# Handing out a feed-forward layer item by item between attention cells, with per-pair loads and weight casts on another engine

## The chip, the cores and the metric

The kernel runs on one core of a Trainium2 chip. The metric is the device time of one execution in microseconds (us). TensorE (PE in the profile) does matrix products, with its weight loads listed apart as PEld; VectorE is DVE, ScalarE is ACT, GpSimd is POOL, and SyncE (SP) issues most of the transfers. SBUF is the memory on the core that the engines read and write, divided into 128 partitions; PSUM is the memory into which TensorE writes its results. Times come from several executions; a profile comes from one execution, and its span is about 2 us shorter than the device time of the same run.

Each run is labelled with a state. On one core a run counts as slow when it is more than 1.5% above the fastest run of the same kernel. Ratios in this document are the mean time of one kernel's fast runs over the mean time of the other kernel's fast runs in the same rounds, so they are not quite the ratio of the medians quoted beside them. Intervals are 95% intervals.

## The reference, cut to what matters

Two layers follow each other. The first is a block-wise linear attention with a decaying state, for 4 batches, 8 heads, 768 positions and head size 64. The second is a dense feed-forward layer over all 3,072 tokens.

```
for b in range(nb):                         # blocks of one sequence, in order
    intra = (qb @ kb^T) * Dmask @ vb         # within the block
    inter = (qb * lam_pow) @ kv_state        # from all earlier blocks
    out[block] = intra + inter
    kv_state = lam_block * kv_state + (kb * rev_pow)^T @ vb

h = x @ w_in                                 # x: 3072 x 512, w_in: 512 x 2048
g = 0.5 * h * (1 + tanh(c * (h + 0.044715 h^3)))
return g @ w_out                             # w_out: 2048 x 512
```

The only serial dependency is `kv_state`, from one block to the next of the same head. Each group of 512 tokens of the feed-forward layer needs all eight heads of its tokens, and nothing else of the attention.

## The kernel before

The kernel uses blocks of 128 tokens (six for each batch) and works on two heads at a time, a "head pair" of 128 partitions (four pairs). I call one block of one head pair a cell; there are 4 x 6 x 4 = 96 cells. Everything is computed in 16-bit floats and accumulated in 32 bits in PSUM. Here `Sps` holds the products of k and q, `PT` is their masked form, `OKV` holds the output and the update of the state, and `xT` is the attention output that the feed-forward layer reads. This is one cell, cut:

```python
Sps = ps_S.tile(...)                               # 2 buffers
# two matmuls: k^T q of each head                  -> Sps
nc.vector.tensor_tensor(PT, Sps, mask, ALU.mult)   # DVE
OKV = ps_OKV.tile([P, P + D], FP32, tag="OKV")     # 2 buffers
for hl in range(2):                                # two heads
    nc.tensor.matmul(OKV[opart, 0:P], a16[v], PT, ...)
    if blk > 0:
        nc.tensor.matmul(OKV[opart, 0:P], kv_prev, qkT, ...)
    nc.tensor.matmul(OKV[opart, P:P+D], a16[k], a16[v], ...)
# DVE: kv32_new, kv_new = decay * kv32_prev + OKV[:, P:P+D]
# ACT: xT[:, hp, tokens] = OKV[:, 0:P]
```

The feed-forward group of 512 tokens has 16 first-layer steps (I call one an item) and four second-layer blocks of 16 matmuls each. `Hps` and `O2ps` are the PSUM results of the two layers, and `gT` holds the activated first layer of a group:

```python
gT = gt_pool.tile([P, NF, GSZ], FP16, tag="gT")    # 16 KiB per partition, 1 buffer
for f in range(16):
    # 4 matmuls 128x128 by 512 columns           -> Hps  (2 PSUM buffers, shared with O2ps)
    # ACT h = Hps;  DVE s = h*h;  DVE u = (s+C)*h;  ACT z = sigmoid(u);  DVE gT[f] = z*h
for tau in range(4):
    # 16 matmuls over gT and w_out               -> O2ps ; ACT o = O2ps ; store
```

And this is the order in which the program hands the work to the engines, cut:

```python
# w_in's 4 MB load is issued first, then q, k, v of batch 0
groups_after_batch = {0: [0], 1: [1, 2], 2: [3], 3: [4, 5]}
for b in range(B):
    qkv_next = load_qkv(b + 1)
    for hp in range(NHP):
        attention_hp(b, hp, *qkv_cur)        # all six blocks of a pair, one after the other
        if b == 0 and hp == 0:
            emit_w_out_load_cast()           # one 4 MB load, 16 casts on ACT
    for g in groups_after_batch[b]:
        emit_moe_group(g)                    # whole groups
```

## Time and profile before

| | before |
|---|---|
| median of 4 runs | 410.97 us (410.69 to 411.7) |
| span of the profiled run | 409.0 us |
| first cell of batches 0, 1, 2 and 3 (its Sps matmul), from the timeline | 31.3, 80.0, 163.7 and 255.2 us |
| last cell | 320.5 us |
| first gT | 114.7 us |
| from the last cell's Sps to the end ("the tail") | 88.4 us |

The page of the profile of the kernel before: busy time of each engine, then the span in 40 slices of about 10.2 us each, a digit being the busy share of the slice in tenths; PEclk is the clock granted to PE in tenths of full speed.

```profile
PE 308.6 (75%) x1696; PEld 144.4 (35%) x1696; DVE 232.0 (57%) x658; ACT 193.5 (47%) x388; POOL 17.5 (4%) x41
...
PE   0015989797278898889987999977988975895585
...
DVE  3023465546289907995389805999044568518840
...
PEclk9999999999999999999999996899995569999999
```

No engine is full on average. PE has three gaps: the start (first three digits), the slice with digit 2 at about 105 us, and the fives in the last quarter. DVE swings between 9 and 0 or 3 from slice to slice. So the kernel is a series of stages with different limits, and not one stage with one limit.

Stretches of the kernel before. Columns: stretch in us, its length, then busy time (and count of instructions) of PE, PEld, DVE, ACT and POOL, the granted PE clock, the busy share of the DMA engines, and GB/s.

```profile
40.00:50.00 10.00, 9.41 (x58) 4.73 (x57) 4.17 (x17) 3.25 (x10) 0.96 (x2) 1.00 1.14 218
100.00:110.00 10.00, 1.38 (x12) 1.05 (x11) 1.65 (x4) 9.51 (x19) 0.78 (x2) 1.00 0.77 157
120.00:130.00 10.00, 8.68 (x53) 4.14 (x51) 9.29 (x26) 6.69 (x15) 0.00 (x0) 1.00 0.00 0
140.00:150.00 10.00, 9.53 (x45) 4.09 (x44) 3.90 (x10) 2.55 (x5) 0.00 (x0) 1.00 0.21 73
310.00:320.00 10.00, 7.86 (x53) 4.32 (x52) 4.89 (x19) 3.07 (x8) 0.00 (x0) 0.50 0.00 0
340.00:350.00 10.00, 5.66 (x24) 2.32 (x24) 8.60 (x18) 6.66 (x12) 0.00 (x0) 1.00 0.01 2
```

At 100–110 us PE stands still while ACT casts w_out. At 120–130 us DVE is the limit, at 140–150 us PE is and DVE idles. At 340–350 us, in the tail, PE has only 24 matmuls (six items) in 10 us, and DVE is 86% busy. At 310–320 us nearly only attention runs (the first wide matmul comes at 319.75 us), and the granted clock is half.

The timeline of PE in the kernel before. Columns: start in us, duration in us, engine, line of the program, operation with output and inputs, shapes; in brackets the idle time before it and what ended it.

```profile
71.86 0.31 PE L174 MATMUL OKV<-qkT,kv_new 64*64 64x128 f16 x1 [0.29 <-DVE kv_new L184]
...
73.42 0.31 PE L174 MATMUL OKV<-qkT,kv_new 64*64 64x128 f16 x1 [0.29 <-DVE kv_new L184]
...
75.91 0.61 PE L203 MATMUL Hps<-xT,w_in 128*128 128x512 f16 x1
...
129.31 0.24 PE L174 MATMUL OKV<-qkT,kv_new 64*64 64x128 f16 x1
...
318.83 0.31 PE L174 MATMUL OKV<-qkT,kv_new 64*64 64x128 f16 x1 [0.29 <-DVE kv_new L184]
```

Consecutive blocks of one pair come every 1.56 us, and each time PE stands 0.29 us until DVE has made the new state. The last two lines give a second reading: the same matmul takes 0.31 us at 72 us and 0.24 us at 129 us, and a wide matmul takes 0.61 us here and 0.38 us later. At 319 us, where the granted clock reads 0.50, it takes 0.31 us again. The Trainium skill, "TensorE: Matmul & The Clock Gate", Part 1, says that the PE clock is at half rate by default (1.2 instead of 2.4 GHz) and that activity releases it. The durations (0.31 and 0.24 us) agree with two such speeds.

Two lines of the waits of the kernel before. Columns: who waits, for whom, us in total, times, longest.

```profile
ACT o L222 <- PE O2ps L219: 56.3, 24, 2.9
...
PE OKV L174 <- DVE kv_new L184: 11.8, 27, 0.9
```

### The profile page before, as it was taken

The page shows a single profiled execution, that of the slowest core. Times are in us where ns is not written, and L with a number is a line of the kernel's source. Part 1 is how long each engine was busy: PE and PEld are TensorE (multiplying, and loading weights), DVE is VectorE, ACT ScalarE, POOL GpSimd, SP SyncE. Part 2 cuts the span into 40 slices and gives each one's busy share as a digit, 9 for nine tenths or more (in the row PEclk, how much of TensorE's full clock was granted, in tenths as well). Part 3 has the DMA queues.
Part 4 walks back from the last instruction along what each step waited for, and adds up shares of the span by engine and source line. Part 5 has one row for each costly group of instructions (what it writes and reads, how often), then busy time and mean ns, then how long its engine had stood idle before and what let it go on. Part 6 is the DMA issues. An engine that isn't in the chain of part 4 may idle for free.

```text
span 409.0 us, 4938 instructions
## 1 busy us (share of the span) xinstructions
PE 308.6 (75%) x1696; PEld 144.4 (35%) x1696; DVE 232.0 (57%) x658; ACT 193.5 (47%) x388; POOL 17.5 (4%) x41
## 2 busy tenths in 40 slices
PE   0015989797278898889987999977988975895585
PEld 0002444353034344344443444343444322342232
DVE  3023465546289907995389805999044568518840
ACT  3512222333967616773467433576133266436641
POOL 1001011101000001000000101010010000000000
PEclk9999999999999999999999996899995569999999
DMA  7999999980950054001100020000200000020002
GB/s 286 283 217 218 218 258 338 220 171 2 207 101 2 1 147 111 0 2 39 63 2 2 3 101 0 2 0 2 78 26 2 0 0 2 26 77 2 2 26 78
DMA packets 24841, 33.87 MB, mean 83 GB/s; under 512 B 752, under 2 KB 19184, under 8 KB 24304
## 3 DMA queue, kind: packets, MB, share of 16 engines
q1 hardware_dynamic: 24816, 33.56, 33.1%
q8 instruction: 13, 0.21, 0.2%
q14 instruction: 12, 0.10, 0.1%
HBM read 27.27 MB, written 6.29 MB: 82 GB/s over the span
## 4 chain that ended last, share of the span: by engine, by line
PE 48%; DVE 21%; issue 11%; ACT 10%; POOLq 0%; POOL 0%; ACTq 0%; DVEq 0%
PE O2ps L219 16%; PE Hps L203 11%; DVE u L211 8%; PE OKV L174 7%; PE OKV L176 6%; DVE s L209 4%; ACT h L207 3%; PE Tps L149 3%; PE OKV L171 3%; ACT z L214 2%; DVE kv_new L181 2%; ACT w_out L120 2%; DVE gT L215 2%; PE Sps L163 2%; DVE PT L166 2%
## 5 line engine op out<-in xcount | busy, mean ns | idle before, releaser
L203 PE MATMUL Hps<-xT,w_in 128*128 128x512 f16 x384 | 104.9, 407 | 23.2 <-ACT h L207 23.0
L219 PE MATMUL O2ps<-w_out,gT 128*128 128x512 f16 x384 | 84.9, 379 | 4.8 <-ACT h L207 3.9
L214 ACT ACTIVATE z<-u 128x512 f16<-128x512 f16 x96 | 59.9, 629 | 45.8 <-DVE u L211 45.7
L211 DVE SCALAR_TENSOR_TENSOR u<-s,h 128x512 f16<-128x512 f16 x96 | 65.4, 692 | 1.2
L203 PEld LDWEIGHTS <-w_in 128*128 128x128 f16 x384 | 36.5, 100 | 67.1 <-issue 33.7
L189 ACT ACTIVATE xT<-OKV 128x128 f16<-128x128 f32 x96 | 26.4, 275 | 70.9 <-DVE kv_new L184 54.4
L207 ACT ACTIVATE h<-Hps 128x512 f16<-128x512 f32 x96 | 56.5, 592 | 6.5 <-PE Hps L203 4.1
L166 DVE TENSOR_TENSOR PT<-Sps,mask_all 128x256 f16<-128x256 f32 x96 | 39.4, 416 | 33.7 <-PE Sps L163 26.0
L171 PE MATMUL OKV<-PT,a 128*64 128x128 f16 x192 | 49.1, 277 | 10.8 <-DVE PT L166 5.4
L219 PEld LDWEIGHTS <-gT 128*128 128x128 f16 x384 | 36.8, 98 | 51.3 <-DVE gT L215 8.0
L209 DVE TENSOR_TENSOR s<-h 128x512 f16<-128x512 f16 x96 | 40.0, 419 | 25.2 <-ACT h L207 24.1
L174 PE MATMUL OKV<-qkT,kv_new 64*64 64x128 f16 x160 | 44.5, 278 | 12.2 <-DVE kv_new L184 11.8
L181 DVE SCALAR_TENSOR_TENSOR kv_new<-kv_new,lam128vec,OKV 128x64 f32<-128x64 f32 x64 | 17.8, 279 | 56.2 <-PE OKV L176 56.1
L149 PE MATMUL Tps<-ident,a 128*128 128x128 f16 x192 | 24.2, 268 | 32.9 <-DVE a L137 22.5
L215 DVE TENSOR_TENSOR gT<-z,h 128x512 f16<-128x512 f16 x96 | 40.7, 424 | 9.8 <-ACT z L214 9.2
L176 PE MATMUL OKV<-a 128*64 128x64 f16 x192 | 42.4, 238 | 0.0
L222 ACT ACTIVATE o<-O2ps 128x512 f32<-128x512 f32 x24 | 14.3, 597 | 56.3 <-PE O2ps L219 56.3
L151 ACT ACTIVATE qkT<-Tps 128x512 f16<-128x512 f16 x48 | 28.1, 600 | 21.6 <-PE Tps L149 21.6
L163 PE MATMUL Sps<-qkT 64*128 64x128 f16 x192 | 23.7, 255 | 12.4 <-ACT qkT L151 10.6
L174 PEld LDWEIGHTS <-kv_new 64*64 64x64 f16 x160 | 18.3, 114 | 38.1 <-DVE kv_new L184 18.7
L149 PEld LDWEIGHTS <-a 128*128 128x128 f16 x192 | 15.7, 118 | 38.1 <-DVE a L137 22.4
L171 PEld LDWEIGHTS <-a 128*64 128x64 f16 x192 | 21.6, 119 | 21.2 <-issue 10.8
(34 smaller groups left out, 131.2 us busy)
## 6 DMA issues: line engine op xcount, KB each, us to landing
out_dram<-o SPq DMA_DIRECT2D x24, 256.0 KB, 2.0
w_in<-in_moe_w_in_dram SPq DMA_DIRECT2D x1, 4096.0 KB, 13.1
w_out<-in_moe_w_out_dram SPq DMA_DIRECT2D x1, 4096.0 KB, 21.7
q<-in_q_dram SPq DMA_DIRECT2D x4, 0.2 KB, 17.9
k<-in_k_dram SPq DMA_DIRECT2D x4, 0.2 KB, 20.4
v<-in_v_dram SPq DMA_DIRECT2D x4, 0.2 KB, 17.1
lam_bc<-in_lam_dram SPq DMA_DIRECT2D x1, 4.0 KB, 2.5
```

Source lines behind the costliest of these rows:

```text
L149: nc.tensor.transpose(Tps[:, bip, t, :], a16[:, t, blk, :, :], ident[:])
L166: nc.vector.tensor_tensor(PT[:], Sps[:, :, 0:P], mask_all[:, h0 : h0 + 2, :], ALU.mult)
L171: nc.tensor.matmul(OKV[opart, 0:P], a16[:, 2, blk, hl, :], PT[:, hl, :], start=True, stop=(blk == 0))
L174: nc.tensor.matmul(OKV[opart, 0:P], kv_prev[opart, :], qkT[opart, blk, 0, :], start=False, stop=True)
L176: nc.tensor.matmul(OKV[opart, P : P + D], a16[:, 1, blk, hl, :], a16[:, 2, blk, hl, :], start=True, stop=True)
L203: nc.tensor.matmul(Hps[:], w_in16[:, c, f * P : (f + 1) * P], xT[:, c, gcol : gcol + GSZ], start=(c == 0), stop=(c == 3))
L207: nc.scalar.activation(out=h16[:], in_=Hps[:], func=AF.Copy)
L209: nc.vector.tensor_tensor(s16[:], h16[:], h16[:], ALU.mult)
L211: nc.vector.scalar_tensor_tensor(u16[:], s16[:], C_ADD, h16[:], ALU.add, ALU.mult)
L214: nc.scalar.activation(out=z16[:], in_=u16[:], func=AF.Sigmoid, scale=C_SIG)
L215: nc.vector.tensor_tensor(gT[:, f, :], z16[:], h16[:], ALU.mult)
L219: nc.tensor.matmul(O2[:], gT[:, f, tau * P : (tau + 1) * P], w_out16[:, f, :], start=(f == 0), stop=(f == NF - 1))
```

## The change

The intent is to let the two layers overlap. While one engine works on an attention cell the others should have a piece of the feed-forward layer to do, and the other way round. Arithmetic, shapes and number of matmuls (1,696) stay. The diff, cut to its core:

```diff
-    at32/at16/atT bufs=2, ptp bufs=3
+    at32/at16/atT/ptp bufs=4          # one set for each head pair
-    gl bufs=2, gt bufs=1
+    gl bufs=4, gt bufs=2
@@ weights
-    w_in load first; 4 casts on ACT; w_out as one load into the same staging, 16 casts on ACT
+    w_in load after q, k, v of batch 0; w_out in four pieces through two buffers
+    def w_steps_gen():                 # one step is handed out per cell of batch 0
+        for c in range(4):
+            yield lambda c=c: nc.gpsimd.tensor_copy(out=w_in16[:, c, :], in_=w_in32[:, c, :])
+        for j in range(4):
+            if j > 0:
+                yield lambda j=j: w_dma_out(j)
+            ...                        # casts of w_out: odd f on ACT, even f on POOL
@@ loads
-    load_qkv(b): three loads of 8 heads
+    load_qkv_hp(b, hp): three loads of 2 heads
@@ emission
-    for hp in range(NHP):
-        attention_hp(b, hp, *qkv_cur)
-    for g in groups_after_batch[b]:    # {0: [0], 1: [1, 2], 2: [3], 3: [4, 5]}
-        emit_moe_group(g)
+    jobs_after = {(0, 5): [(0, GSZ)],       (1, 1): [(GSZ, GSZ)],
+                  (1, 5): [(2 * GSZ, GSZ)], (2, 3): [(3 * GSZ, GSZ)],
+                  (3, 1): [(4 * GSZ, GSZ)], (3, 5): [(5 * GSZ, GSZ)]}
+    # a job is 16 first-layer items and 4 second-layer items; it is admitted
+    # as soon as block `blk` of batch `b` is finished for all four pairs
+    for b in range(B):
+        for hp in range(NHP):
+            prep_hp(b, hp, ...)        # decay scaling, transposes
+            pump(2)                    # emit two feed-forward items
+        ...                            # loads of batch b+1
+        for blk in range(NBLK):        # blocks outside,
+            for hp in range(NHP):      # head pairs inside
+                st = cell_start(b, blk, hp)        # Sps of this cell
+                finish_cell(previous)              # PT, OKV, state, xT of the one before
+                if b == 0: one step of the weights
+                pump(1)                            # emit one feed-forward item
+    pump(all)
```

## The prediction

> What bounds the kernel now. No one engine: the page gives PE 75%, DVE 57%, ACT 47%. The table of stretches shows serial stages.
> - 0–30 us, start: PE starts at 22.4 us. The 4 MB w_in transfer is first, then 256-byte-packet q, k, v at about 218 GB/s.
> - 30–101 us, attention only. In the timeline consecutive blocks of one head pair repeat every 1.56 us: PE OKV waits for DVE kv_new. The PE work inside is about 1.18 us.
> - 101–109 us: 16 ACT casts of w_out (8.3 us in the chain); PE nearly idle.
> - 110–330 us, alternation: first-layer phases with DVE 90–97% busy (1.43 us per f: s, u, gT), then 14 us blocks of 64 O2ps matmuls with DVE nearly idle (gT has one buffer).
> - 330–409 us: two whole groups alone, PE 55% in their first-layer phases, 79 us.
>
> What the change does. Arithmetic and shapes stay. It (1) loads batch 0 per head pair, ahead of w_in; (2) walks blocks outside and head pairs inside, so that the kv chain has four cells in which to finish; (3) doubles gT, has four gl buffers and hands MoE out one item per cell; (4) moves w_in casts and half of w_out's to POOL, w_out in four pieces.
>
> Costs, estimated from durations in the trace.
> - PE work: 768 wide matmuls at 0.217 us = 167; 96 cells, 1.18 us each, less about 7 for first blocks = 106; 192 transposes at 0.135 = 26. Together 299 us.
> - Start: 4.7 MB at 218 GB/s, first cell near 26 us (before: 31).
> - Batch 0 cells: 24 x 1.2 us, to 56 us.
> - Handover to MoE: gl and gT reuse staging memory, so the first gT waits for the last w_out piece. w_in lands near 45 us; POOL casts it in about 4 x 2.9 us (scaled from 0.54 us for 384 columns), then issues the last two w_out pieces, beside batch 1's loads: near 77 us. Four f items get ahead, and DVE stands in order behind. Twelve items and prep follow: batch 1's cells start near 97 us. The Trainium skill, "SBUF — State Buffer", says that POOL and DVE share a port pair under an exclusive lock; no run here shows yet what this costs the casts.
> - Batch 1, 2, 3 cells with 128 to 150 wide matmuls each: 58–60 us each, PE-bound. Prep of batches 2 and 3: 21 and 23 us.
> - Tail: 40 O2ps (9), 16 first-layer items at 1.43 (24), 64 O2ps (14), store (3): 50 us instead of 79.
> Sum 366 us. I add 10 for waits where engines run in a compiled order and both PE and DVE are full; the old stages of that kind filled about 95%.
>
> Nearly all is on the critical path: the wins are the tail (29), the attention chain (15–20), the cast block (8) and the O2ps blocks that now overlap; the handover gives some 20 back.
>
> Predicted 376 us, 80% range 352 to 398. Faster by over 2%: 0.90; within 2%: 0.08; slower: 0.02.
>
> Right if: PE share rises above 80% from 100 to 320 us; the waits no longer list ACT o on O2ps or OKV on kv_new; DVE busy time stays near 232 us; wide matmuls alone fill only the last 50 us; between 56 and 97 us DVE gT waits for POOL or DMA.
>
> Wrong if: POOL's casts are several times slower under the lock, or ACT casts hold up xT behind a late load (slower); the hole is small (faster); the granted clock, 0.5 around 310–330 us before, drops over long stretches (up to 20 us slower).

## The result, and the profile after

| | before | after |
|---|---|---|
| median | 410.43 us (16 runs, 409.62 to 411.7) | 355.42 us (11 runs, 352.7 to 361.08) |
| ratio of fast runs | | 0.8643 [0.8617, 0.867] |

The changed kernel is 13.6% faster. The one profile that was taken with this result was slow (span 359.3 us, mean granted clock 0.962; three of the 11 runs were slow). I therefore ran the changed kernel once more beside the later experiments, as same_again, and read its profile, which is fast: span 355.9 us, mean granted clock 0.976. All fences "after" are from it.

> The changed kernel unchanged, for a profile in the fast state beside the other runs of this job: 352 to 356 us if fast, and milestones within a few us of the slow profile (batch 1's first cell near 92 us, last cell near 300 to 309 us).

It gave 354.62 us (353.08 to 357.72), ratio 0.8632 [0.857, 0.8693].

The page of the profile after. The slices are about 8.9 us each now.

```profile
PE 302.2 (85%) x1696; PEld 140.1 (39%) x1696; DVE 226.5 (64%) x658; ACT 180.9 (51%) x376; POOL 35.3 (10%) x56
...
PE   0437879957899999899988999987999988999795
...
DVE  3426445667973468892888860799934888508940
...
PEclk9999999988999989999999978999999999999999
```

From the eleventh slice on PE shows 8 and 9 almost throughout; its share from 100 to 310 us is 93.7%. The digit 2 of the kernel before and the fives of its last quarter are gone, except in the very last slice. The granted clock of this profile has no 5 and 6 any more; the slow profile of the same kernel still has one 5.

Stretches of the kernel after, with the same columns as before.

```profile
40.00:50.00 10.00, 7.97 (x46) 4.10 (x47) 4.47 (x17) 1.54 (x6) 7.75 (x7) 1.00 1.17 221
70.00:80.00 10.00, 5.25 (x28) 2.17 (x26) 6.10 (x17) 7.81 (x15) 0.96 (x2) 0.83 1.11 201
100.00:110.00 10.00, 9.80 (x61) 4.68 (x60) 7.23 (x23) 3.60 (x9) 0.00 (x0) 1.00 0.00 0
190.00:200.00 10.00, 9.10 (x53) 4.22 (x53) 8.64 (x26) 6.30 (x14) 0.00 (x0) 1.00 0.00 1
280.00:290.00 10.00, 9.11 (x53) 4.11 (x52) 8.58 (x25) 6.24 (x14) 0.00 (x0) 1.00 0.00 1
330.00:340.00 10.00, 7.99 (x35) 3.31 (x35) 10.00 (x25) 8.56 (x16) 0.00 (x0) 1.00 0.01 2
```

At 190 and 280 us PE is 91% busy and DVE is 86% busy in the same stretch: the two limits that took turns before (120–130 and 140–150 us) are now met together. At 40–50 us POOL does the casts (7.75 us), which ACT did before. The weak stretch is 70–80 us. In the tail, at 330–340 us, PE has 35 matmuls instead of 24, and DVE has no gap.

Where the time came from can be read as PE idle time by stretch (span minus busy time, summed from the table of stretches):

| stage | before | after (same_again) | saved |
|---|---|---|---|
| start (0–30 us in both) | 29.2 | 20.4 | 8.8 |
| up to the steady part (30–110 before, 30–90 after) | 21.3 | 11.4 | 9.9 |
| middle (110–330, 90–310) | 26.8 | 14.5 | 12.3 |
| tail (330–409, 310–355.9) | 23.0 | 7.4 | 15.6 |
| PE busy time | 308.6 | 302.2 | 6.4 |
| span | 409.0 | 355.9 | 53.1 |

The rows sum to the span within rounding. This tells where PE idled less. It does not tell which part of the change did it; the experiments try to do that.

### The profile page after: what moved, and what is told of

Same layout as the page of the kernel before. It is cut to its first block, busy times and chain, and to the rows that moved or that the text cites. A ratio compares the mean times of both kernels' runs of the same rounds, so it can differ in the third digit from the quotient of the medians.

```text
span 359.3 us, 4945 instructions
## 1 busy us (share of the span) xinstructions
PE 305.8 (85%) x1696; PEld 141.5 (39%) x1696; DVE 226.8 (63%) x658; ACT 180.9 (50%) x376; POOL 35.2 (10%) x56
## 4 chain that ended last, share of the span: by engine, by line
PE 66%; DVE 13%; ACT 12%; SPq 5%; issue 2%; DMA 2%; ACTq 0%; DVEq 0%
PE O2ps L264 24%; PE Hps L244 15%; PE OKV L210 8%; PE OKV L212 7%; PE OKV L207 6%; ACT h L248 4%; PE Sps L192 3%; DVE gT L257 3%; ACT qkT L176 3%; DVE u L252 3%; DVE s L250 3%; ACT z L255 2%; DMA k<-in_k_dram 2%; SPq L148 2%; SPq L144 2%
## 5 line engine op out<-in xcount | busy, mean ns | idle before, releaser
L264 PE MATMUL O2ps<-w_out,gT 128*128 128x512 f16 x384 | 96.0, 395 | 2.4 <-ACT h L248 1.5
L248 ACT ACTIVATE h<-Hps 128x512 f16<-128x512 f32 x96 | 56.7, 597 | 29.4 <-DVE gT L257 14.2
L255 ACT ACTIVATE z<-u 128x512 f16<-128x512 f16 x96 | 59.8, 630 | 10.8 <-DVE u L252 8.9
L225 ACT ACTIVATE xT<-OKV 128x128 f16<-128x128 f32 x96 | 26.3, 276 | 71.9 <-DVE kv_new L220 50.6
L244 PEld LDWEIGHTS <-w_in 128*128 128x128 f16 x384 | 34.2, 100 | 55.7 <-issue 27.6
L264 PEld LDWEIGHTS <-gT 128*128 128x128 f16 x384 | 35.8, 101 | 45.6 <-issue 7.6
L207 PE MATMUL OKV<-PT,a 128*64 128x128 f16 x192 | 46.5, 263 | 7.3 <-ACT xT L225 5.7
L210 PE MATMUL OKV<-qkT,kv_new 64*64 64x128 f16 x160 | 41.9, 262 | 0.0
L174 PE MATMUL Tps<-ident,a 128*128 128x128 f16 x192 | 22.6, 254 | 21.1 <-DVE a L163 15.0
L212 PE MATMUL OKV<-a 128*64 128x64 f16 x192 | 40.5, 227 | 0.0
L167 POOL CAST a<-v 128x384 f16<-128x384 f32 x32 | 19.6, 644 | 176.7 <-PE OKV L212 150.0
L176 ACT ACTIVATE qkT<-Tps 128x512 f16<-128x512 f16 x48 | 26.9, 599 | 17.5 <-PE Tps L174 17.1
L267 ACT ACTIVATE o<-O2ps 128x512 f32<-128x512 f32 x24 | 14.0, 597 | 41.2 <-PE O2ps L264 41.2
L207 PEld LDWEIGHTS <-a 128*64 128x64 f16 x192 | 20.2, 112 | 34.3 <-issue 15.0
L212 PEld LDWEIGHTS <-a 128*64 128x64 f16 x192 | 20.1, 114 | 14.2 <-issue 1.0
## 6 DMA issues: line engine op xcount, KB each, us to landing
wo<-in_moe_w_out_dram SPq DMA_DIRECT2D x1, 1024.0 KB, 19.2
```

What stands on the lines that cost most here:

```text
L174: nc.tensor.transpose(Tps[:, bip, t, :], a16[:, t, blk, :, :], ident[:])
L207: nc.tensor.matmul(OKV[opart, 0:P], a16[:, 2, blk, hl, :], PT[:, hl, :], start=True, stop=(blk == 0))
L210: nc.tensor.matmul(OKV[opart, 0:P], kv16[hp][opart, :], qkT[opart, blk, 0, :], start=False, stop=True)
L212: nc.tensor.matmul(OKV[opart, P : P + D], a16[:, 1, blk, hl, :], a16[:, 2, blk, hl, :], start=True, stop=True)
L244: nc.tensor.matmul(Hps[:, 0:n], w_in16[:, c, f * P : (f + 1) * P], xT[:, c, t0 : t0 + n], start=(c == 0), stop=(c == 3))
L248: nc.scalar.activation(out=h16[:, 0:n], in_=Hps[:, 0:n], func=AF.Copy)
```

## The experiments

The prediction named five causes: the attention chain, the tail, the cast block at 101–109 us, second-layer blocks that overlap, and, as a loss, a "handover" hole in front of the first feed-forward group. My theory was that each of them is worth about what the prediction gave it. The rivals were that some of them were worth nothing, because what they wait for is hidden anyway, and that the granted clock decides. Each experiment undoes or adds one part. Unless told otherwise, an experiment starts from the changed kernel, which takes 354–355 us.

### Late admission of the groups (jobs_late), and the old walk besides (hp_outer_late)

```diff
 jobs_late:
-  (1, 1): [g1], (1, 5): [g2], (2, 3): [g3], (3, 1): [g4], (3, 5): [g5]
+  (1, 5): [g1, g2], (2, 5): [g3], (3, 5): [g4, g5]     # as the kernel before
 hp_outer_late, in addition:
-  for blk in range(NBLK):
-      for hp in range(NHP):
+  for hp in range(NHP):
+      for blk in range(NBLK):
```

> The changed kernel with one edit: the table that admits MoE groups is put back to batch ends (group 0 after batch 0, 1 and 2 after batch 1, 3 after batch 2, 4 and 5 after batch 3). Theory A (most of the gain is the shorter tail, won because groups are admitted by block row while attention still runs): two whole groups run alone after the last attention cell, some 79 us as before the change instead of 50, so about 25 to 30 us slower than the changed kernel, 380 to 385 us. Rival B (the gain is in the start, the weight casts and the buffers; admission time matters little): within 8 us of the changed kernel, under 364 us.

> As jobs_late, and the walk is put back too: head pairs outside, blocks inside. To be compared with jobs_late, since that walk could not admit groups by row anyway. Theory of the prediction (four cells of distance break the kv chain, worth 15 to 20 us): 15 to 20 us slower than jobs_late. Rival (the two OKV buffers pace the cells in both walks; in batch 0 of the changed trace two cells take about 3.5 us, so 1.77 us a cell, where the old walk took 1.56): within 6 us of jobs_late, perhaps faster.

jobs_late took 365.28 us (363.32 to 370.04), ratio 0.8893 [0.8847, 0.8939]. So early admission is worth some 10 us, between the two ranges that I had expected (25 to 30, or under 8). The profile of jobs_late, of a run in the slow state, shows two effects: with two groups left after the last cell instead of one the tail is 68.9 us instead of 50.2, but the last cell comes 6.3 us earlier (299.4 instead of 305.7). A longer tail is thus not lost in full.

hp_outer_late took 361.87 us (358.2 to 363.62), ratio 0.8796 [0.8744, 0.8847]. It is not slower than jobs_late; if anything it is 1% faster. In its profile (of a slow run) PE OKV again waits for DVE kv_new, mostly 0.29 us at a time as in the kernel before, though only for 5.2 us in 17 waits, and the time does not suffer. With the items handed out between cells, the new walk gave nothing by itself, where the prediction had given the attention chain 15–20 us. The walk over blocks outside is still needed, but for another reason: only with it is a group of tokens complete before its batch has ended, so that it can be admitted early.

### The two kinds of feed-forward buffers (one_gt, one_gt_only, before_two_gt)

```diff
 one_gt:        gl bufs 4 -> 2 and gT bufs 2 -> 1
 one_gt_only:   gT bufs 2 -> 1
 before_two_gt: the kernel BEFORE with gl bufs 2 -> 4 and gT bufs 1 -> 2
```

> The changed kernel with gT back to one buffer and the h, s, u, z pool back to two. If double buffers are what lets O2ps blocks overlap first-layer work: 15 us slower or more, 370 us up. If the one-item-per-cell order already does the overlapping and buffers only help at group borders (my theory): 3 to 10 us slower, 358 to 366 us.

> The changed kernel with gT back to one buffer alone; the pool of h, s, u, z keeps four. one_gt (both back) took 375.7 us, some 20 more than the changed kernel. Theory A (the O2ps block holds the only gT, so the next group's first layer has to wait): nearly all of the 20 comes back here, 370 us or more. Theory B (two h, s, u, z buffers make each f item wait for a round through ACT and DVE, 1.67 us an item in the tail of one_gt, where four let DVE run without gaps at about 1.3): at most 8 us slower, 358 to 363 us, and the tail's first-layer phase is as short as in the changed kernel.

> The kernel before with two numbers changed: gT two buffers, h, s, u, z pool four. If the buffers are worth 20 us by themselves in any order of work, 385 to 393 us. If they need the new order (items handed out between cells) to pay, 400 us or more. If they pay more here, because two whole groups stand alone at the end and 220 us are first-layer phases, under 383 us.

one_gt took 375.68 us (375.3 to 378.62), ratio 0.9178 [0.9143, 0.9212], so 21 us longer, where my theory had said 3 to 10. one_gt_only took 354.05 us (351.3 to 355.61), ratio 0.8622 [0.8572, 0.8672], the same as the changed kernel. So the second gT buffer, 16 KiB of each partition, buys nothing that can be measured here, and the four small buffers for h, s, u and z buy the 21 us: one_gt and one_gt_only differ in them alone. (One thing came along with the single gT: its first write no longer waited for a cast of w_out and came at 70.1 us instead of 77.1. no_hole, below, shows that this by itself is worth little.) One stretch of the tail shows how; first one_gt, then one_gt_only, with the columns of the stretches above.

```profile
340.00:350.00 10.00, 5.30 (x24) 2.10 (x23) 8.36 (x18) 6.87 (x12) 0.00 (x0) 1.00 0.01 2
```

```profile
320.00:330.00 10.00, 8.25 (x35) 3.29 (x34) 10.00 (x25) 9.40 (x17) 0.00 (x0) 1.00 0.01 2
```

With two buffers six items are done in 10 us, with DVE at 84%, and this is the rate of the kernel before (24 matmuls and 18 DVE instructions at 340–350 us there). With four buffers DVE is full and about eight items are done. The period of an item in the tail before, 1.67 us, was a wait for buffers, and not the work of DVE, which needs 1.25 us.

before_two_gt took 407.89 us (406.91 to 408.74), ratio 0.9941 [0.9911, 0.9971]. The same buffers are worth 2 us there instead of 21. Its page (granted clock alone) and two of its stretches show why.

```profile
PEclk9999999999999995999999655589965556999999
```

```profile
230.00:240.00 10.00, 8.89 (x53) 4.34 (x53) 5.44 (x22) 1.65 (x6) 0.18 (x2) 0.50 0.00 1
310.00:320.00 10.00, 8.30 (x53) 4.37 (x53) 6.21 (x22) 3.07 (x8) 1.08 (x2) 0.50 0.01 2
```

Its tail is 73.5 us instead of 88.4, so 15 us were won. But the groups finish sooner, and then attention cells stand alone for longer, at a granted clock of 0.50 at 230–260 and 300–340 us. The mean granted clock is 0.88 against 0.95 before, and PE is busy for 326.5 us with the matmuls that took 308.6. The gain went into stretches where PE runs slowly, most of them on narrow matmuls.

### The items handed out all at once (pump_all)

This keeps everything else: the early admission, the buffers, the weights, the loads, the walk. Only, an admitted group is emitted at once, as the kernel before does.

```diff
-  pump(2)        # after each prep
+  pump(1000)
-  pump(1)        # after each cell
+  pump(1000)
```

> The changed kernel with one thing undone: admitted MoE items are emitted all at once instead of two per prep and one per cell. Theory (wide matmuls handed out between cells keep PE filled during the cells' waits and keep its clock up; a stretch of cells alone runs at half clock and at the pace of the OKV buffers): stretches of cells alone come back after batch 0, with granted clock 0.5 or small-matmul durations of 0.31 us instead of 0.24, and the time is 12 to 25 us longer, 366 to 380 us. Rival (the compiled order interleaves well enough by itself once there are four h, s, u, z buffers): within 6 us of the changed kernel.

It took **405.84 us** (404.13 to 406.77), ratio 0.9863 [0.9805, 0.9921]. Nearly the whole gain is gone, 51 of 55 us, two to four times the 12 to 25 that I had expected, although the tail is even shorter (41.4 us instead of 50.2). The page of pump_all (busy times and granted clock), two of its stretches, and PE's timeline:

```profile
PE 337.0 (83%) x1696; PEld 155.6 (38%) x1696; DVE 225.7 (56%) x658; ACT 184.4 (46%) x376; POOL 32.8 (8%) x56
...
PEclk9999999899856998559997555999555899656999
```

```profile
160.00:170.00 10.00, 8.08 (x47) 4.19 (x46) 4.44 (x18) 1.57 (x6) 0.00 (x0) 0.50 0.00 1
230.00:240.00 10.00, 8.64 (x48) 4.29 (x47) 4.75 (x18) 1.67 (x6) 0.00 (x0) 0.50 0.01 2
```

```profile
166.59 0.32 PE L207 MATMUL OKV<-PT,a 128*64 128x128 f16 x1 [0.68 <-ACT xT L225]
...
168.22 0.31 PE L210 MATMUL OKV<-qkT,kv_new 64*64 64x128 f16 x1
```

In these stretches cells run alone, about six in 10 us. PE's share looks high, 81% and 86%, but each narrow matmul takes 0.31–0.32 us, the half-clock duration. Over the whole span PE is busy for 337.0 us with the same 1,696 matmuls that took 302.2 us in same_again: 34.8 us of the difference are the same matmuls taking longer (the mean granted clock is 0.827 against 0.976), and 14.3 us are more idle time (68.0 against 53.7). The sum is the whole difference of the two spans, 405.0 − 355.9 = 49.1 us. How much of the 49 us is the clock itself and how much is that a lone cell has nothing to hide its waits behind was not separated.

Two places of the Trainium skill help to read this. "Perfetto Trace Analysis", § Identifying the Most-Contended Engine, says that the busy share of matmuls is a poor measure of how near PE is to its limit. This agrees: the page gives PE 83% for pump_all and 85% for the changed kernel, and between them lie 51 us. (That page's reason is that matmuls are pipelined; here the same matmuls also last longer.) In the same page, § Optimization Strategy says of kernels whose most-contended engine changes over time that "performance may be improved by interleaving those regimes". This is the change in one sentence, and pump_all is its measurement, given all the other parts of the change. The hand-out alone, added to the kernel before with its old buffers, weights and admission, was not run.

### The old order of weights and loads (weights_old)

```diff
+ w_in load issued before q, k, v of batch 0; w_in cast on ACT
+ w_out as one load into w_in's staging buffer, 16 casts on ACT, emitted at the 4th cell
- w_out in four pieces, casts shared by POOL and ACT, one step per cell
```

> The changed kernel with the old handling of weights: w_in transferred ahead of q, k, v and cast on ACT; w_out in one 4 MB transfer into the same staging buffer, cast by 16 ACT instructions, emitted after the first row of cells. Prediction: the start costs about 5 us more (first cell at 31 us instead of 26) and the ACT cast block about 8: 13 us slower or so, near 367 us. Rival (the late MoE start hides behind batch 0's cells and loads): under 5 us slower. If w_in cast earlier lets MoE start earlier it could even be faster.

It took 374.89 us (373.27 to 376.79), ratio 0.9145 [0.9112, 0.9177], so 20 us longer, where I had expected 13. Two stretches of its profile:

```profile
90.00:100.00 10.00, 7.96 (x47) 4.18 (x45) 4.68 (x18) 1.67 (x6) 0.00 (x0) 1.00 1.01 173
110.00:120.00 10.00, 6.12 (x25) 2.41 (x24) 3.18 (x9) 8.92 (x18) 0.00 (x0) 1.00 0.00 0
```

The first cell starts at 36.5 us instead of 26.3, and the feed-forward layer starts (its first h) at 114 us instead of 66. Until then the cells of batch 1 run ahead alone (90–100 us: six xT copies on ACT, 47 narrow matmuls, DVE 47%), and ACT does the w_out casts at 105–114 us. The milestones place the loss: batch 1's first cell is even earlier (84.6 us instead of 92.6), batch 2's is 17.7 us later and the last cell 19.2 us later. So the loss is not the 8 us of the casts alone, and it arises while batch 1 runs. My reading is that the feed-forward layer has fewer cells left to be interleaved with. This run puts back the order of the loads, the single transfer and the engine of the casts together; which of them costs how much was not separated.

### No wait of gT for the last piece of w_out (no_hole)

In the changed kernel gT lies in memory that the staging buffers of the weights used, so the first write to it waits for the last cast of w_out. Here the pools are laid out so that gT reuses only w_in's staging.

```diff
+ gl and o32 pools are allocated up front, w_out's staging is kept for the whole kernel
  wi32 (w_in's staging) is opened last and closed after batch 0: gT takes its place
```

> The changed kernel with the memory of the h, s, u, z and o32 pools set aside from the start, and gT laid over the w_in staging alone, so that the first gT no longer waits for the casts of the last w_out piece. Prediction (the handover costs some 20 us against a dense start): PE's idle time between 66 and 92 us shrinks, 5 to 12 us faster than the changed kernel, 344 to 350 us. Rival (ACT, whose queue holds w_out casts, qkT copies and h, z in a fixed order, and batch 1's loads are the limit there): under 3 us gained.

It took 353.56 us (352.0 to 354.64), ratio 0.8626 [0.86, 0.8652], against 0.8632 for same_again and 0.8643 for the first result. That is 0.2 to 0.7 us, and the intervals overlap, so no gain is shown. Three lines of the waits of the changed kernel (columns as before) give its size, and answer to the lines shown of the kernel before:

```profile
ACT xT L225 <- DVE kv_new L220: 49.0, 47, 4.3
...
ACT o L267 <- PE O2ps L264: 41.2, 18, 4.8
...
DVE gT L257 <- ACT w_out L132: 2.7, 1, 2.7
```

The third line is the handover: one wait of 2.7 us. Without it the first gT came at 70.0 us instead of 77.1, but batch 1's first cell only 1.2 us earlier (91.4 instead of 92.6). What else limits the weak stretch of 65–92 us was not isolated: ACT is busy for 21.4 of the 27 us, PE for 20.0 and DVE for 19.6, with 13 items and the preparation of four pairs, beside batch 1's loads. A small part of the DVE time is interference. DVE and POOL at 66–68 us of the changed kernel:

```profile
66.59 0.87 DVE L250 TENSOR_TENSOR s<-h 128x512 f16<-128x512 f16 x1 [2.16 <-ACT h L248]
67.14 1.61 POOL L167 CAST a<-v 128x384 f16<-128x384 f32 x2
...
67.50 0.88 DVE L252 SCALAR_TENSOR_TENSOR u<-s,h 128x512 f16<-128x512 f16 x1
```

Beside POOL's casts, s takes 0.87 us instead of its usual 0.42, u takes 0.88 instead of 0.68, and the two v casts take 0.80 us each on average instead of 0.48 (at 25 us, beside nothing). The Trainium skill, "SBUF — State Buffer", § Who interferes with whom, says that DVE and GpSimd share a pair of memory ports under an exclusive lock, and that a DVE instruction with two inputs in SBUF contends with a GpSimd instruction that reads SBUF. The trace agrees: s and u have two such inputs here. Of the 15 s and u instructions that overlap one of POOL's, 7 are slowed, by 0.2 to 0.45 us each and about 2 us in all; none of the other 177 is. The w_in casts took 1.89 us each, where the prediction had estimated 2.9 by scaling a shorter cast.

### Four OKV buffers (okv4)

In batch 0 the changed kernel's cells run alone. PE's timeline in same_again:

```profile
30.99 0.31 PE L207 MATMUL OKV<-PT,a 128*64 128x128 f16 x1 [0.69 <-ACT xT L225]
31.23 0.31 PE L210 MATMUL OKV<-qkT,kv_new 64*64 64x128 f16 x1
...
34.51 0.32 PE L207 MATMUL OKV<-PT,a 128*64 128x128 f16 x1 [0.68 <-ACT xT L225]
...
102.05 0.24 PE L210 MATMUL OKV<-qkT,kv_new 64*64 64x128 f16 x1
```

The wait for DVE kv_new is gone from PE's list, as intended. But PE now waits 0.68 us after every second cell for ACT's xT copy, because there are only two OKV buffers and each is held until xT has been copied. The copy in its turn waits for DVE (49.0 us of waits in the first of the lines above): both read the same OKV buffer, which lies in one PSUM bank, and the compiled program puts these two reads one after the other. The Trainium skill, "PSUM — Partial Sum Buffer", § PSUM bank collisions raise a hardware error, says that two engines must not access one bank in the same partitions at the same time and that software has to keep them apart; no run here tried it otherwise.

```diff
-  psS bufs=2 (of two banks each), psOKV bufs=2
+  psS bufs=1, psOKV bufs=4; the transposes' Tps tile comes from the OKV buffers
```

> The changed kernel with PSUM dealt out otherwise: one Sps buffer of two banks instead of two, and OKV and Tps share four one-bank buffers instead of OKV having two. Theory (two OKV buffers, held until xT has been copied, pace batch 0's cells at about 1.63 us each): the cells of batch 0 go faster, toward the 1.2 us of their matmuls at the half clock that the durations show there, so that stage takes about 30 us instead of 39. End to end 2 to 6 us less than the changed kernel, since MoE still waits for w_in and w_out. Rival (something else paces the cells, such as the single Sps or the half clock itself): the stage keeps 37 us or more and the time is equal or longer.

This gave 348.5 us once and 355.86, 354.49 and 355.11 us in runs labelled slow (granted clock 0.951 to 0.956). PE's timeline of it:

```profile
30.59 0.31 PE L207 MATMUL OKV<-PT,a 128*64 128x128 f16 x1
...
31.97 0.31 PE L207 MATMUL OKV<-PT,a 128*64 128x128 f16 x1
```

This shows what the waits of batch 0 cost. They are gone (PE has no gap from 29.5 to 57 us), a cell takes 1.38 us (31.97 − 30.59) instead of 1.76 (half of 34.51 − 30.99), and the last xT of batch 0 comes at 57.1 us instead of 65.4. Not all of these 8 us is the faster pace: since Tps no longer takes Sps buffers, the first Sps comes at 11.5 us, during the preparation, instead of 26.3. What is left of them at the end can't be said, with one run fast. The narrow matmuls still take 0.31 us, although PE has no gap.

### Useless wide matmuls in batch 0 (warm)

If the half clock comes from the narrow cells alone, then extra wide matmuls should raise it.

```diff
+  if b == 0 and blk < NBLK - 1:        # after PT of each cell; the result is thrown away
+      for i in range(4):
+          nc.tensor.matmul(dummy[:, 0:256], ident, PT, start=True, stop=True)
```

> The changed kernel with four useless 256-column matmuls per cell in batch 0 (all but its last row), written to a PSUM buffer that nobody reads; results stay right. Theory (PE runs at half clock in batch 0 because cells alone keep too little of the array busy, whatever the page's granted clock of 1.00 says): the small matmuls there go from 0.31 to 0.24 us and wide ones from 0.61 to 0.38, and the stage does not get longer although 1024 columns per cell were added, within 4 us of the changed kernel end to end. Rival (the half clock comes from elsewhere, such as time since start): durations stay 0.31, each cell gets 0.85 us longer on PE, the stage grows by some 10 us and the time by 3 to 10.

PE's timeline of it in batch 0:

```profile
41.97 0.24 PE L215 MATMUL OKV<-qkT,kv_new 64*64 64x128 f16 x1
...
42.80 0.61 PE L207 MATMUL dummy<-PT,ident 128*128 128x256 f16 x4
```

The narrow matmul takes 0.24 us instead of 0.31, so the clock is raised, with more work. Batch 0 ended at 63.5 us instead of 65.4, although 1,024 columns more per cell went through the array. A cell with its useless work takes 1.55 us, and PE is busy for 29.97 of the 30 us from 30 to 60. So the two OKV buffers alone do not hold a cell to 1.76 us: at half clock a cell is 1.38 us of matmuls (okv4) and 0.38 us of waiting for them. The profiled run took 359.43 us (fast); the three others took 366.28, 369.41 and 374.44 us. Their mean granted clocks (0.963 to 0.990) are not below the fast run's 0.962. Only the first has a trace, so why the others are so much slower stays open.

### An attempt at a faster version (best)

```diff
+  okv4's buffers
-  (3, 5): [(5 * GSZ, GSZ)]
+  (3, 3): [first 256 tokens of group 5], (3, 5): [last 256 tokens]
-  pump(1)
+  pump(2 if b == B - 1 else 1)
```

> The changed kernel with okv4's PSUM layout, the last group split into two of 256 tokens, the first of them admitted after block row 3, and two items per cell in batch 3. If PE is the limit in the cell stages and only the tail wastes it (16 first-layer items alone at DVE's pace, then 64 O2ps with DVE idle), the tail after the last cell shrinks from 50 us to about 28 while the cells of batch 3 take 10 to 13 us longer: 338 to 346 us. If splitting costs as much as it saves (twice the weight loads, fixed cost of 256-column instructions on DVE and ACT), 346 us or more.

It took 354.86, 351.46, 360.47 and 361.29 us. Its tail is 32 us instead of 50, but the cells of batch 3 take longer (its last cell comes at 321.1 us instead of 305.7), and a stretch has a granted clock of 0.50. That stretch, and PE's timeline in it:

```profile
260.00:270.00 10.00, 10.00 (x41) 3.85 (x42) 4.98 (x14) 2.03 (x6) 0.00 (x0) 0.50 0.00 0
```

```profile
263.40 1.46 PE L244 MATMUL Hps<-xT,w_in 128*128 128x512 f16 x3
264.79 0.29 PE L192 MATMUL Sps<-qkT 64*128 64x128 f16 x2
265.01 0.31 PE L207 MATMUL OKV<-PT,a 128*64 128x128 f16 x1
```

PE is busy all the time and has wide matmuls after each cell, and is still at half clock: some wide matmuls between cells do not lift the clock in every case. The version is not better than the changed kernel; of the two ranges expected, it is the second that came (346 us or more). No run beats the changed kernel clearly; one_gt_only equals it with 16 KiB less memory per partition.

## Why the prediction was right or wrong

The prediction of 376 us, with 352 to 398, held 354–355 us near its lower end, and the direction was right. The reasons were right in part, and some of the sums came out right by luck.

**Right: the stages.** The milestones that follow from its text, against same_again:

| | predicted | measured |
|---|---|---|
| first cell | 26 | 26.3 |
| end of batch 0's cells (24th xT) | 56 | 65.4 |
| first gT | 77 | 77.1 |
| batch 1's first cell | 97 | 92.6 |
| batch 2's first cell | 176 | 169.4 |
| batch 3's first cell | 259 | 248.5 |
| last cell | 319 | 305.7 |
| tail | 50 | 50.2 |

The stage figures add up to 369 us (319 + 50), where the text says 366. The measured span is 355.9 us. The tail's agreement is luck in part: after the start of the last cell, second-layer matmuls and the rest of the cells took 14.1 us ("40 O2ps (9)"; 52 were left), the last first layer 18.0 ("16 first-layer items at 1.43 (24)"; about 1.1 each), the last 64 O2ps 14.2 and the store 3.9. The two errors cancel.

**Mis-sized: the PE work of a cell.** The text has "96 cells, 1.18 us each" throughout. At full clock a cell's eight matmuls take 1.00 us: in same_again the next work after those that start at 101.88 us starts at 102.88 us. At half clock they take 1.38 us (okv4). The one figure was too large for batches 1 to 3, whose stages came 2.2, 3.9 and 2.8 us shorter than predicted, and too small for batch 0, where "24 x 1.2 us" became 39 us (26.3 to 65.4) and the two OKV buffers added their waits. The first gT came at the predicted time all the same, since it waited for w_out. Whether the 9 us longer stage cost anything at the end stays open (okv4).

**Covered by another error: the margin.** "I add 10 for waits where engines run in a compiled order and both PE and DVE are full" was not needed on top. From 92.6 to 305.7 us PE idled for 14.1 us. The cell's work was put too high by about 13 us there (an estimate: 72 cells, 1.18 − 1.00 us each), and the three stages together came only 8.9 us shorter than predicted. So some 4 us of waits came that the stages did not have, and the too large cell hid them. That is luck.

**Right milestone, wrong worth: the handover.** "the first gT waits for the last w_out piece" was right: without that wait the first gT came at 70.0 us instead of 77.1 (no_hole). What failed is "the handover gives some 20 back". Without the wait batch 1's first cell came 1.2 us earlier and the end 0.2 to 0.7 us, within the noise, and PE idles for only about 7 us in all at 65–92 us. What else holds this stretch was not isolated.

**Wrong: the attribution.** "the attention chain (15–20)" is refuted by hp_outer_late: with the old walk back and the items still handed out, nothing was lost. In the kernel before, the wait that it names is 11.8 us in all. Removing the wait on kv_new only handed it to the next wait, OKV for xT (6.1 us in same_again). "the tail (29)" by early admission is worth 10 us of the end-to-end time (jobs_late): it shortens the tail by 19 us but brings the last cell 6 us later. That the tail itself measures 50.2 us rests on the buffers too (tail 59.8 us in one_gt). "the cast block (8)" was too small: the old order of weights and loads costs 20 us, though not by the casts alone (weights_old). And "the O2ps blocks that now overlap", which stands last and has no number, is the largest: handing out the items one by one is worth 51 us, given all the rest (pump_all).

**Why these do not add.** Undoing one part costs 10 (jobs_late), 21 (one_gt), 20 (weights_old) or 51 us (pump_all). The sum is 102 us, and the whole gain is 55. Each undoing destroys overlap that the others also need. From the other side, buffers alone gave the kernel before 2 us (before_two_gt), and everything except the hand-out gave it 4 (pump_all: 405.84 against 410.17). A sum of gains is the wrong form for such a change; the sum of stages, which the prediction also made, is what came out right.

**The signs it named.** PE share above 80% from 100 to 320 us: yes (93.7% to 310). DVE busy near 232 us: yes (226.5). Wide matmuls alone only in the last 50 us: yes. "the waits no longer list ACT o on O2ps": wrong, it is still there with 41.2 us (56.3 before), and PE hardly waits in turn (PE O2ps on ACT o: 0.5 us, once). It was a badly chosen sign. "or OKV on kv_new": yes, and a new wait took its place. "DVE gT waits for POOL or DMA" between 56 and 97 us: it waited for ACT's last w_out cast, once, 2.7 us.

**The clock.** The prediction feared half-clock stretches as a risk of up to 20 us. In the fast profile of the changed kernel no slice is below 7, where the kernel before had two fives and two sixes; the slow profile has one 5. They come back when the mixing of wide and narrow matmuls is taken away (pump_all; before_two_gt, which never had it). That the mixing is what keeps the clock up is my reading: warm agrees, but best at 260–270 us shows 0.50 with both kinds mixed.

## What to carry to other kernels

When the profile shows two engines taking turns at being full, hand out the work of both stages in small pieces in turn, on every cell; here, undoing the pieces cost more than undoing early admission, the deeper buffers or the walk that breaks the dependency chain, and PE's mean granted clock was higher with them (0.976 against 0.827). Cost such a change by walking through its stages with the limit of each, and not by adding up gains. Before paying for a big buffer, test it alone: here the 16 KiB one was worth nothing, and the small ones were worth 21 us in the new order.

## What the Trainium skill lacked or had wrong

- "TensorE: Matmul & The Clock Gate", Part 1, puts the half clock down to PE idle for a window of about 3.4 us, or to idle gaps between groups with which the clock swings to and fro. It says that the clock follows how busy PE has been, but not what counts as busy. The runs show a lasting 0.50 without such gaps: PE is busy for all 10.00 us at 260–270 us of best, and at 222–232 us of pump_all its longest gap is 0.69 us. Most such stretches have only narrow matmuls (64 or 128 columns). In batch 0 such cells stay at 0.31 us a matmul without any gap (okv4, 29.5–57 us), and four 256-column matmuls per cell lift them to 0.24 us (warm). But at 260–268 us of best one to three 512-column matmuls after each cell did not lift them. The page lacks that a PE without gaps can stay at half rate; what decides it stays open.
- The same page: the clock column of the profile reads 1.00 in stretches near the start where the durations show half (0.31 and 0.61 us against 0.24 and 0.38 us at 129 us in the kernel before). The page says to distrust single clock events; that the time before the first drop can read as full speed is not in it.
- "SBUF — State Buffer", § Who interferes with whom, gives the lock and two probed slowdowns, but no size for a mixed stretch of engine work. Here it was 0.2 to 0.45 us for each slowed s or u on DVE (7 of the 15 that overlapped POOL), and 0.3 us on average for the two POOL casts of 384 columns at 67 us.
- "PSUM — Partial Sum Buffer", on bank collisions, does not say what keeping two readers of one bank apart costs: here ACT's copy waited for DVE's two reads (49.0 us in 47 waits), and PE, which needs one of two OKV buffers to come free after that copy, waited 0.68 us after every second cell of batch 0. How much of the 0.68 us is due to the order of the reads was not tried.
- No page says that the gains of parts of an interleaving change don't add: here 102 us of single losses against a gain of 55 us.
